# A Fourier-mixing and cosine-gated feed-forward kernel: a weight load issued once instead of twice, two last sums on GpSimd, and other queues for the last stores

## The chip, the cores and the metric

The kernel runs on one core of a Trainium2 chip. The metric is the device time of one execution in microseconds (us); the median of several executions is compared. All data are float32.

The core has a matrix engine (TensorE; PE in the profile, and PEld for its loads of weights), a vector engine (VectorE, DVE), an activation engine (ScalarE, ACT), GpSimd (POOL) and SyncE (SP), which here only issues transfers. Transfers (DMAs) are issued from the queues of SyncE, ScalarE and GpSimd, each of which goes through its instructions in order, waits included.

## The reference

```python
x: (8, 3008, 256); w_in: (256, 2048); w_out: (2048, 256)
X = np.fft.fft(x, axis=1)
X = np.fft.fft(X, axis=2)
x = X.real.reshape(24064, 256)
h = x @ w_in
g = h * np.cos(h)
out = g @ w_out
```

## The kernel before

Each of the 8 batches goes through two parts. The **transform** computes the Fourier transform over the sequence (3008 = 47 x 64) in two matrix stages. The first stage (`first_half`, eight chunks of columns) leaves its result in tiles `zs`, which `store_z` writes to a scratch array `zd` in memory; `load_z` brings it back in another order as `z`, and `second_half` multiplies that by a table `BJ` (matmuls into `pb`, line 528). The transform over the feature axis is not done on the tokens: it is folded into the weights. `fold_weights` multiplies the input weights by cosine and sine tables (matmuls into `pw`, line 597), `keep_fold` copies the result into `WC` and `WS`, and `turn_row` turns one row of it into a column by four matmuls of one column each (`pt`, line 629). The weights `w_in` are folded in four quarters of 512 columns, each once for cosine and once for sine.

The **feed-forward** part goes in steps of 256 tokens by 256 hidden columns: six token groups for each batch, eight steps in each. A step has matmuls with the folded weights (`mm1`, line 712, two halves `e`), rounding and a sine on ScalarE with VectorE around them for `h * cos(h)`, and matmuls with the output weights (`mm2`, line 803) that add up over the eight steps of a group. The steps are laid out by hand as a pipeline (`LAG` = 3): in turn `t` of the main loop one step starts, and the three before it are further along. Symmetry halves the work: a token and its mirror image are computed together, and the output weights are first combined into sums and differences (`w2_sums`). So `mm2` leaves seven partial results in the accumulators, and sums of them give the results of the tokens and of their mirrors. For all groups but the last these sums run on GpSimd (`combine_m`, by `add`, line 855) in later turns; a 32x32 block transpose on VectorE and `store_out` (line 910) write them out, first half `sg` = 0, then `sg` = 1.

The order of the work is the order of the calls; each engine's queue is in program order. The stretches around the change:

- **Head.** SyncE issues, in this order: the tables and the first quarter of `w_in`, the input of batch 0, part of `BJ`, then `load_w(1)`, `load_w2(0, 2)`, and `load_w(2)` twice (lines 273 to 277; the transfer is line 226, into the tile `wr`). Behind these in the same queue follow the stores of the first stage for chunks 4 to 7 (`store_z`, line 505; chunks 0 to 3 are on GpSimd's queue, and one store on ScalarE's), `load_z(0, 0)` (line 514), the rest of the output weights, the last quarter of `w_in`, the second set of stores and its load, and the rest of the tables. TensorE's order is: the eight chunks of the first stage, the folds of quarter 1 (sine, cosine), `turn_row(1)`, the sine fold of quarter 2, `second_half(0, 0)`; then the first feed-forward step (`seed_first`, line 698, matmuls with a single row; `mm1`; `spread_norm`, line 556, also a single row), in between the cosine fold of quarter 2. From the second token group on, a row of each group's transform goes to memory (`nd`, line 548) and comes back spread over all partitions (`nb`, line 549); ScalarE's `seed` (line 682) starts each step from it.
- **Tail.** `combine_last` does the sums of the very last group on VectorE (lines 867 to 874). `store_last` then transposes the results on TensorE (line 884) and copies them out (887 and 888); for each half `sg` it issues four stores (line 892). Just before that, in turn `n + 1`, `store_out(..., late=True)` issues the eight stores of the second half of the group before: four from SyncE, four from GpSimd.

Of the kernel before, what the change touches and what calls it, by code (L numbers as in the profile page):

```python
# [13 lines left out]
ALU = mybir.AluOpType  # L14
# [98 lines left out]
def _cols(g):  # L113

    if g == 0:
        return [(1, 64, 0), (2, 64, 64), (3, 64, 128), (0, 33, 192)]
    return [(4 * g + q, 64, 64 * q) for q in range(4)]


def _runs(g, sg):  # L120


    runs = []
    for j, n, c in _cols(g):
        a, k = c, 0
        if sg:
            a, j = 256 - c - n, (N2 - j) % N2
            if j == 0:
                a, k, n = a + 1, 33, 31
        runs.append((a // 32, j, k, n))  # L130
    return runs
# [3 lines left out]
def kernel(  # L135
# [7 lines left out]
    nc = tc.nc  # L143
# [79 lines left out]
    def load_w(q):  # L223
        cols = slice(512 * q, 512 * q + 512)
        if q < 3:
            nc.sync.dma_start(
                out=staged[q][:, 0:1024].rearrange("p (i f) -> p i f", i=2),
                in_=moe_w_in.rearrange("(i p) f -> p i f", p=128)[:, :, cols],
            )
            return  # L230
        for i in range(2):
            nc.sync.dma_start(out=wr[q][i], in_=moe_w_in[128 * i : 128 * i + 128, cols])
# [10 lines left out]
    def load_w2(f0, f1):  # L243
        nc.sync.dma_start(
            out=w2.rearrange("p (q c) -> p q c", c=ND)[:, 2 * f0 : 2 * f1],
            in_=moe_w_out.rearrange("(q p) c -> p q c", p=128)[:, 2 * f0 : 2 * f1],
        )
# [25 lines left out]
    load_bj(0, 512)  # L273
    load_w(1)
    load_w2(0, 2)
    load_w(2)
    load_w(2)
    WC = cpool.tile([128, NDFF], FP, tag="WC", name="WC")
    WS = cpool.tile([128, NDFF], FP, tag="WS", name="WS")
# [15 lines left out]
    def psum(name, tag="fft"):  # L295
        return ppool.tile([128, 512], FP, tag=tag, bufs=bank[tag], name=name)
# [297 lines left out]
    def fold_weights(e, n, tag="M"):  # L594
        pw = psum("pw", tag)
        for i in range(2):
            nc.tensor.matmul(  # L597
                pw,
                lhsT=CS[i][:, 128 * e : 128 * e + 128],
                rhs=wr[n][i],  # L600
                start=(i == 0),
                stop=(i == 1),
            )
        return e, n, pw
# [249 lines left out]
    def add(o, a, b, less):  # L854
        return nc.gpsimd.tensor_tensor(  # L855
            out=o, in0=a, in1=b, op=ALU.subtract if less else ALU.add
        )

    def combine_last(s):
        key = (s.b, s.grp)  # L860
        M5, M3 = acc[key][2], acc[key][3]
        mv = mrs.pop(key).rearrange("p (m t) -> p m t", m=7)
        outs[key] = spool.tile([128, 7 * 256], FP, tag="cb", bufs=1, name="cb")
        cv = outs[key].rearrange("p (m t) -> p m t", m=7)
        tt, stt = nc.vector.tensor_tensor, nc.vector.scalar_tensor_tensor
        more = dict(op0=ALU.mult, op1=ALU.add)
        tt(out=cv[:, 0], in0=mv[:, 0], in1=mv[:, 1], op=ALU.add)
        stt(out=cv[:, 4], in0=M5[:, 256:512], scalar=-TWO_PI, in1=mv[:, 0], **more)
        stt(out=cv[:, 6], in0=M5[:, 0:256], scalar=TWO_PI, in1=cv[:, 4], **more)
        stt(out=cv[:, 1], in0=M3[:, 0:256], scalar=TWO_PI, in1=cv[:, 6], **more)  # L870
        store_last(s, 0)
        tt(out=cv[:, 5], in0=cv[:, 4], in1=mv[:, 3], op=ALU.add)
        tt(out=cv[:, 2], in0=cv[:, 5], in1=mv[:, 2], op=ALU.add)
        stt(out=cv[:, 3], in0=M5[:, 0:256], scalar=TWO_PI, in1=cv[:, 5], **more)
        store_last(s, 1)

    def store_last(s, sg):
        cv = outs[s.b, s.grp].rearrange("p (m t) -> p m t", m=7)
        ob = spool.tile([128, 512], FP, tag="zs", bufs=4, name="ob")
        ov = ob.rearrange("t (h c j) -> t h j c", h=2, j=2)  # L880
        pos = [psum("po", "H").rearrange("t (z j c) -> t z j c", z=2, j=2)[:, 0] for _ in "ab"]
        for j in range(2):
            for h in range(2):
                nc.tensor.transpose(
                    pos[h][:, j], cv[:, 2 * sg + j, 128 * h : 128 * h + 128], ident
                )
        nc.scalar.copy(out=ov[:, 0], in_=pos[0])
        (nc.vector.tensor_copy if sg else nc.scalar.copy)(out=ov[:, 1], in_=pos[1])
        queues = (nc.sync, nc.sync, nc.scalar if sg else nc.gpsimd, nc.sync if sg else nc.gpsimd)
        for queue, (t0, j, k, m) in zip(queues, sorted(_runs(s.grp, sg))):  # L890
            h, r0 = divmod(32 * t0, 128)
            queue.dma_start(
                out=out_r[s.b, j, k : k + m, :],
                in_=ob[r0 : r0 + m, 256 * h : 256 * h + 256],
            )

    def store_out(s, sg, late=False):
        ob = spool.tile([128, 512], FP, tag="ob", bufs=2, name="ob")
        ov = ob.rearrange("p (t c) -> p t c", c=64)
        nc.vector.transpose(  # L900
            out=ov.rearrange("p t (c j) -> p j t c", j=2),
            in_=outs[s.b, s.grp][:, 512 * sg : 512 * sg + 512],
        )
        for t0, j, k, n in _runs(s.grp, sg):
            to = out_r[s.b, j].rearrange("k (q c) -> q k c", c=64)
            for i in range(0, n, 32):
                m = min(32, n - i)
                src, dst = ov[:, t0 + i // 32], to[:, k + i : k + i + m]
                if m == 32:
                    (nc.gpsimd if late and i else nc.sync).dma_start(out=dst, in_=src)  # L910
                    continue
                for q in range(4):
                    nc.sync.dma_start(out=dst[q], in_=src[32 * q : 32 * q + m])
# [6 lines left out]
    for b in range(NB):  # L920
        for g in range(NG):
            for fp in range(8):
                s = Step()
# [59 lines left out]
    n = len(steps)  # L983
# [10 lines left out]
    late = fold_weights(0, 2)  # L994
# [37 lines left out]
    for t in range(LAG, n + LAG + 1):  # L1032
# [6 lines left out]
        if t - LAG - 1 == n - 1:  # L1039
            combine_last(steps[n - 1])  # L1040
            break
# [38 lines left out]
        if step(t - LAG - 4, True):  # L1080
            store_out(step(t - LAG - 4), 0)
        if step(t - LAG - 5, True):
            if t == n - 1:
                todo.setdefault(n + 1, []).append((store_out, step(t - LAG - 5), 1, True))
            else:
                store_out(step(t - LAG - 5), 1)
# [34 lines left out]
```

## Time and profile before

| what | value |
|---|---|
| runs (three) | 1946.1, 1946.07, 1945.48 us; median 1946.07 |
| profiled execution, device time | 1945.86 us |
| its span in the trace | 1944.1 us |
| mean granted TensorE clock | 0.996 |
| busy: PE, PEld, DVE, ACT, POOL | 99%, 87%, 92%, 79%, 22% of the span |
| DMA | 89.87 MB, mean 46 GB/s |

Times in the profile are in us from the start of the span. The device time of the profiled execution is 1.8 us more than its span. A line of a timeline reads: start, duration, engine and source line, operation, written tile and read tiles, shape, count; in brackets the engine's idle time before it and what ended that. An engine with a q (SPq) is the queue that issues a transfer, not the transfer. The chain of waits is the work that ended last, followed back from the end: each piece is what the next one waited for. A matmul of a float32 tile is executed as several instructions, so four lines "x4" may stand for two calls.

### The profile page before, as it was taken

How to read it: one execution, taken by the hardware profiler on the slowest of the kernel's cores; microseconds unless marked ns; L12 is line 12 of the kernel's file. 1: busy time of each engine (PE TensorE's matmuls, PEld its weight loads, DVE VectorE, ACT ScalarE, POOL GpSimd, SP SyncE). 2: the span in 40 equal slices, each digit the busy share in tenths (PEclk: the TensorE clock that was granted, in tenths of full speed). 3: DMA queues.
4: the chain of work that ended last, by engine and by line, in shares of the span. 5: the costliest groups of instructions: out<-in, count | busy, mean ns of one | idle time of the engine just before them, and what ended most of it. 6: DMA issues, size and time to landing. Idle time of an engine off the chain costs nothing.

```text
span 1944.1 us, 30503 instructions
## 1 busy us (share of the span) xinstructions
PE 1927.7 (99%) x9508; PEld 1692.3 (87%) x9508; DVE 1780.3 (92%) x3337; ACT 1533.4 (79%) x2888; POOL 419.1 (22%) x507
## 2 busy tenths in 40 slices
PE   8999999999999999999999999999999999999998
PEld 4888899888998889988898888988889888898887
DVE  4899999999899998999989999899999999999998
ACT  3788878888788787888878788788877888788775
POOL 3522202222022211222112221122211222111101
PEclk8999999999999999999999999999999999999999
DMA  6321130012200121011211122110231100110000
GB/s 208 100 62 40 46 89 24 22 37 75 58 22 22 46 75 48 25 26 47 82 36 27 25 56 79 29 30 20 56 85 30 26 20 24 55 28 10 12 22 23
DMA packets 157864, 89.87 MB, mean 46 GB/s; under 512 B 106751, under 2 KB 151478, under 8 KB 155234
## 3 DMA queue, kind: packets, MB, share of 16 engines
q1 hardware_dynamic: 155853, 85.89, 16.4%
q0 software_dynamic: 1728, 1.95, 0.4%
q8 instruction: 76, 1.25, 0.3%
q14 instruction: 87, 0.70, 0.1%
q10 hardware_dynamic: 120, 0.08, 0.0%
HBM read 50.59 MB, written 37.27 MB: 45 GB/s over the span
## 4 chain that ended last, share of the span: by engine, by line
PE 97%; SPq 1%; DVE 1%; DMA 1%; ACT 0%; issue 0%; POOL 0%; POOLq 0%; DVEq 0%; ACTq 0%
PE M L803 58%; PE H L712 34%; PE pb L528 2%; PE pz L420 2%; SPq L196 1%; DMA wr<-in_moe_w_in_dram 1%; PE pw L597 0%; PE pz L357 0%; PE M L420 0%; PE pz L408 0%; ACT r L743 0%; DVE S L768 0%; DVE r L747 0%; DVE r L757 0%; ACT r L753 0%
## 5 line engine op out<-in xcount | busy, mean ns | idle before, releaser
L803 PE MATMUL M<-S,VX 128*128 128x256 f32 (+1 forms) x2304 | 612.3, 375 | 0.0
L803 PEld LDWEIGHTS M<-S,VX 128*128 128x128 f32 x2304 | 437.8, 190 | 49.9
L743 ACT ACTIVATE r<-H 128x512 f32<-128x512 f32 (+1 forms) x384 | 226.2, 589 | 262.0 <-DVE h L728 260.2
L753 ACT ACTIVATE r<-r 128x1024 f32<-128x1024 f32 (+1 forms) x384 | 394.7, 1028 | 22.3 <-DVE r L747 17.1
L712 PE MATMUL H<-pq,WC 128*128 128x256 f32 (+1 forms) x1536 | 394.9, 380 | 1.0 <-ACT H L682 1.0
L712 PE MATMUL H<-pq,WS 128*128 128x256 f32 (+1 forms) x1536 | 388.9, 376 | 0.3 <-ACT ew L723 0.3
L803 PE MATMUL M<-r,w 128*128 128x256 f32 (+1 forms) x1536 | 387.8, 375 | 0.0
L682 ACT ACTIVATE H<-nb,wn 128x256 f32<-128x256 f32 (+1 forms) x766 | 362.5, 473 | 16.2 <-DVE r L757 1.3
L728 DVE TENSOR_TENSOR h<-ew,H 128x512 f32<-128x512 f32 (+1 forms) x384 | 259.1, 675 | 100.8 <-PE H L712 63.1
L712 PEld LDWEIGHTS H<-pq,WC 128*128 128x128 f32 x1536 | 284.1, 190 | 52.3 <-ACT r L743 16.7
L803 PEld LDWEIGHTS M<-r,w 128*128 128x128 f32 x1536 | 300.2, 196 | 28.3 <-issue 0.5
L712 PEld LDWEIGHTS H<-pq,WS 128*128 128x128 f32 x1536 | 291.8, 190 | 34.6 <-ACT ew L723 1.3
L747 DVE SCALAR_TENSOR_TENSOR r<-r,H 128x512 f32<-128x512 f32 (+1 forms) x384 | 258.7, 674 | 26.3 <-ACT r L743 9.7
L855 POOL TENSOR_TENSOR cb<-cb,mr 128x256 f32<-128x256 f32 (+3 forms) x188 | 158.4, 853 | 521.2 <-DVE S L778 483.0
L723 ACT ACTIVATE ew<-H 128x512 f32<-128x512 f32 (+1 forms) x384 | 225.7, 588 | 56.3 <-PE H L712 47.7
L757 DVE SCALAR_TENSOR_TENSOR r<-H,r 128x512 f32<-128x512 f32 (+1 forms) x384 | 256.2, 667 | 3.9 <-ACT r L753 3.3
L747 DVE SCALAR_TENSOR_TENSOR r<-r,h 128x512 f32<-128x512 f32 (+1 forms) x384 | 259.5, 676 | 0.0
L768 DVE TENSOR_TENSOR S<-r 128x512 f32<-128x512 f32 (+1 forms) x384 | 259.1, 675 | 0.1
L757 DVE SCALAR_TENSOR_TENSOR r<-h,r 128x512 f32<-128x512 f32 (+1 forms) x384 | 258.6, 673 | 0.0
L743 ACT ACTIVATE r<-h 128x512 f32<-128x512 f32 (+1 forms) x384 | 236.2, 615 | 0.0
L803 PE MATMUL M<-S,w 128*128 128x256 f32 (+1 forms) x768 | 226.0, 376 | 0.6 <-DVE S L778 0.6
L319 POOL TENSOR_TENSOR xs<-xp 113x512 f32<-113x512 f32 x112 | 143.0, 1277 | 386.7 <-DVE S L778 383.4
(114 smaller groups left out, 1602.9 us busy)
## 6 DMA issues: line engine op xcount, KB each, us to landing
out_dram<-ob SPq DMA_DIRECT2D x724, 32.0 KB
xp<-in_x_dram SPq DMA_DIRECT2D x250, 56.0 KB
z<-zd SPq DMA_DIRECT2D x8, 1280.0 KB
zd<-zs SPq DMA_DIRECT2D x224, 40.0 KB
nb<-nd SPq DMA_DIRECT2D x40, 128.0 KB
zd<-zs SPq DMA_DIRECT2D x224, 8.0 KB
xp<-in_x_dram SPq DMA_DIRECT2D x52, 48.0 KB
wr<-in_moe_w_in_dram SPq DMA_DIRECT2D x4, 512.0 KB
```

The source lines that it names most:

```text
L319: return nc.gpsimd.tensor_tensor(out=xs2[e][0:XL], in0=xv[:, 0], in1=xv[:, 1], op=ALU.subtract if e else ALU.add,)
L682: nc.scalar.activation(out=s.H[:, u * T : u * T + T], in_=s.nb[:, 0:T], func=AF.Copy, bias=0.25, scale=wn[:, f : f + 1],)
L712: nc.tensor.matmul(s.H[:, u * T : u * T + T], lhsT=W[:, 128 * f : 128 * f + 128], rhs=s.pq[:, e * T : e * T + T], start=False, stop=True, ...
L723: nc.scalar.mul(out=s.ew[:, 0 : 2 * s.T], in_=s.H[:, 0 : 2 * s.T], mul=2.0)
L728: return nc.vector.tensor_tensor(out=s.h[:, 0 : 2 * T].rearrange("p (u t) -> p u t", u=2)[:, :, ::-1], in0=s.ew[:, 0 : 2 * T].rearrange("p ...
L743: nc.scalar.activation(out=r, in_=h, func=AF.Copy, bias=BIG, scale=1.0)
L747: nc.vector.scalar_tensor_tensor(out=r, in0=r, scalar=-BIG, in1=h, op0=ALU.add, op1=ALU.subtract)
L753: nc.scalar.activation(out=r, in_=r, func=AF.Sin, bias=0.0, scale=SIN_SCALE)
L757: nc.vector.scalar_tensor_tensor(out=r, in0=h, scalar=-0.25, in1=r, op0=ALU.add, op1=ALU.mult)
L768: return nc.vector.tensor_tensor(out=sv[:, 0:2], in0=gv[:, 2:3].to_broadcast([128, 2, T]), in1=gv[:, 0:4:3], op=ALU.subtract,)
L803: nc.tensor.matmul(acc[key][m // 2][:, 256 * (m % 2) : 256 * (m % 2) + T], lhsT=w, rhs=a, start=first, stop=s.fp == 7, skip_group_check=True,)
L855: return nc.gpsimd.tensor_tensor(out=o, in0=a, in1=b, op=ALU.subtract if less else ALU.add)
```

## The change

Three things are changed. The third quarter of the weights (`load_w(2)`) is requested once, not twice. In `combine_last` two of the sums (`cv[:, 5]` and `cv[:, 2]`) are done by GpSimd, and stand ahead of two VectorE sums in the program. The stores at the end come from other queues: of the last four (`sg` = 1) one from SyncE, two from ScalarE and one from GpSimd, instead of three from SyncE and one from ScalarE; of the eight late stores of `store_out` two from GpSimd and six from SyncE, instead of four and four.

```diff
     load_w(1)
     load_w2(0, 2)
-    load_w(2)
     load_w(2)
@@ combine_last
         tt(out=cv[:, 0], in0=mv[:, 0], in1=mv[:, 1], op=ALU.add)
         stt(out=cv[:, 4], in0=M5[:, 256:512], scalar=-TWO_PI, in1=mv[:, 0], **more)
+        add(cv[:, 5], cv[:, 4], mv[:, 3], False)
+        add(cv[:, 2], cv[:, 5], mv[:, 2], False)
         stt(out=cv[:, 6], in0=M5[:, 0:256], scalar=TWO_PI, in1=cv[:, 4], **more)
         stt(out=cv[:, 1], in0=M3[:, 0:256], scalar=TWO_PI, in1=cv[:, 6], **more)
         store_last(s, 0)
-        tt(out=cv[:, 5], in0=cv[:, 4], in1=mv[:, 3], op=ALU.add)
-        tt(out=cv[:, 2], in0=cv[:, 5], in1=mv[:, 2], op=ALU.add)
         stt(out=cv[:, 3], in0=M5[:, 0:256], scalar=TWO_PI, in1=cv[:, 5], **more)
         store_last(s, 1)
@@ store_last
-        queues = (nc.sync, nc.sync, nc.scalar if sg else nc.gpsimd, nc.sync if sg else nc.gpsimd)
+        queues = (nc.sync, nc.scalar, nc.scalar, nc.gpsimd) if sg else (nc.sync,) * 2 + (nc.gpsimd,) * 2
@@ store_out
-        for t0, j, k, n in _runs(s.grp, sg):
+        for run, (t0, j, k, n) in enumerate(_runs(s.grp, sg)):
...
-                    (nc.gpsimd if late and i else nc.sync).dma_start(out=dst, in_=src)
+                    (nc.gpsimd if late and i and run < 2 else nc.sync).dma_start(out=dst, in_=src)
```

## The prediction

> **What bounds the kernel now.** I read the page first, then the chain of waits in order of time, SyncE's own waits, the timelines of the head and of the tail, and the granted clock in stretches. Lines of the page:
>
> ```profile
> span 1944.1 us, 30503 instructions
> PE 97%; SPq 1%; DVE 1%; DMA 1%; ACT 0%; issue 0%; POOL 0%; POOLq 0%; DVEq 0%; ACTq 0%
> ```
>
> The second line is the chain that ended last: TensorE holds 97% of it, and the change leaves its matmuls alone. So it can only act where the chain leaves TensorE, at the head (SyncE and two weight loads) and after the last matmul, and on the clock at which TensorE runs. The chain at the head (start, us, what):
>
> ```profile
> 18.20 7.79 DMA wr<-in_moe_w_in_dram
> 26.05 3.69 DMA wr<-in_moe_w_in_dram
> 29.88 3.65 PE pw L597 x4
> ...
> 34.73 1.14 PE pb L528 x8
> ...
> 36.70 1.82 PE H L698 x4
> 38.52 1.80 PE H L712 x4
> 40.31 1.04 PE pn L556 x2
> 41.36 1.80 PE H L712 x4
> 43.16 3.43 PE pw L597 x4
> ...
> 49.39 1.04 PE H L712 x4
> ```
>
> The third quarter is loaded twice in a row, and the second load starts only when the first has landed (18.20 + 7.79 = 25.99). The matmuls that fold that quarter (L597) start at 29.88, after the second landing (26.05 + 3.69 = 29.74). What SyncE waited for, and what it issued:
>
> ```profile
> SPq L226 <- DMA wr<-in_moe_w_in_dram: 7.3, 1, 7.3
> SPq L505 <- DMA wr<-in_moe_w_in_dram: 1.1, 1, 1.1
> ```
>
> ```profile
> 18.20 8.22 SPq L226 DMA_DIRECT2D wr<-in_moe_w_in_dram  x2
> 26.52 3.55 SPq L505 DMA_DIRECT2D zd<-zs  x7
> 31.75 0.35 SPq L514 DMA_DIRECT2D z<-zd  x1
> ```
>
> SyncE's queue is in order, so behind the repeated load stand seven stores of the first transform (`zd`), and behind these the load `z` that the first second-half matmuls (`pb`, L528) read. One of the stores waits 1.1 us more for a weight load. From the last store's issue (26.52 + 3.55 = 30.07) to the load of `z` are 1.68 us, from that load to `pb` 2.98 us. The profile gives "issue" as releaser of `pb`; that it is the landing of `z` is my inference, because its other operand was requested long before.
>
> **The change at the head.** Removing the repeated load takes away 7.3 us of SyncE's wait. What comes next in that queue was ready earlier:
>
> ```profile
> 24.80 0.19 ACT L479 COPY zs<-mid 64x4 f32<-64x4 f32 x1
> ```
>
> ```profile
> 27.71 1.05 PE L629 MATMUL pt<-ones,nrow 1*128 1x1 f32 x8
> 52.95 1.88 PE L597 MATMUL pw<-xs,LCS 128*128 128x512 f32 x4
> ```
>
> The last of the stores' data is ready at 24.99 (24.80 + 0.19). The last store can go at about 25.0, or at 26.0 if it still waits for the one weight load; with some 0.35 us of issue, 1.68 and 2.98 us, `pb` can read `z` between 30.0 and 31.0. The fold need no longer wait for a second landing: it follows the eight small matmuls of L629 at 27.71 + 1.05 = 28.76, and at the pace of the row at 52.95 it lasts 1.85, to 30.6. So `pb` starts between 30.6 and 31.0 instead of 34.73; I take 30.95, **3.8 us earlier**. If `z` isn't what `pb` waits for, this term shrinks towards the 29.88 - 28.76 = 1.1 us of the fold's own wait.
>
> The second term is the clock. The same four matmuls of L597 take 3.65 and 3.43 us in the chain, and 1.88 at 52.95; four of L712 take 1.80, and 1.04 at 49.39. Stretches of the grid on which the granted clock changes (us; busy of PE, PEld, DVE, ACT, POOL; then PEclk):
>
> ```profile
> 12.88:16.29 3.41, 2.40 (x16) 1.45 (x16) 3.05 (x6) 0.53 (x2) 0.00 (x0) 1.00 0.64 168
> 26.53:29.94 3.41, 2.29 (x12) 1.25 (x10) 1.82 (x5) 0.84 (x2) 0.00 (x0) 1.00 0.62 183
> 29.95:33.35 3.40, 3.40 (x4) 1.00 (x4) 0.43 (x2) 0.00 (x0) 0.00 (x0) 0.50 0.09 14
> 33.36:36.77 3.41, 1.37 (x10) 1.04 (x9) 1.04 (x3) 1.17 (x2) 0.00 (x0) 1.00 1.00 334
> 36.78:40.18 3.40, 3.40 (x8) 2.20 (x8) 1.29 (x4) 0.00 (x0) 0.00 (x0) 0.50 0.83 250
> 40.19:43.59 3.40, 3.40 (x8) 2.34 (x8) 0.72 (x2) 1.45 (x3) 0.00 (x0) 0.50 0.66 190
> 43.60:47.01 3.41, 3.41 (x6) 1.62 (x5) 1.45 (x3) 1.42 (x3) 3.06 (x10) 0.50 0.58 170
> ```
>
> The clock changes at borders 3.41 us apart, by the work of the stretch before. If the small matmuls (one column in L629, one row in L698 and L556) are not counted, the stretches that lost full clock held 1.2 us (35%, an earlier fold up to 27.71) and 1.37 us (40%); the one at 12.88 kept it with 2.40 less a few tenths of small ones (60 to 70%). At half clock 36.78 (3.40 less L698's 1.8: 50%) and 40.19 (less L556's 1.04: 70%) did not bring it back, 29.95 and 43.60 (all full) did. With the change the stretch at 26.53 holds 1.2 + 1.2 us of fold, 69%: no fall at 29.94. That at 29.95 holds 0.66 of fold and 1.13 of `pb`, 53%, between a share that fell and one that held. So the clock may fall at 33.36. At stake are the five chain pieces from 36.70 to 46.6, 1.82 + 1.80 + 1.04 + 1.80 + 3.43 = 9.89 us at half clock, about 4.95 saved at full clock. If it falls at 33.36, L698 (0.83 us after `pb`'s end, at 32.9) ends at 34.4, the two L712 and L556 at 39.0, and the fold at 41.4 or 42.5, as the clock rises at 40.18 or 43.6: against 46.59 a gain of 5.2 or 4.1. If a fall comes later it costs less, if it doesn't come the gain is 8.7. Nothing in the trace ties the borders to the kernel's start, so I take the middle of the cases with one fall: 3.8 + 2.2 = **6.0 us** (4.1 to 8.7).
>
> On the clock the Trainium skill ("TensorE: Matmul & The Clock Gate", "Why this matters for your kernels") has a rule: full clock is lost after an idle window, so gaps under about 3 us are harmless. By it the changed head, whose longest gap is under 2 us, would hold full clock and the head would give 8.7. The trace disagrees in part: the fall at 29.94 came after a gap of 1.12 us behind 1.05 us of one-column matmuls.
>
> What is late next: all other loads of this phase stand on the same queue and move up with `z`. The tightest one later that I found is the row for the second token group:
>
> ```profile
> 73.28 0.35 SPq L549 DMA_DIRECT2D nb<-nd  x1
> 76.91 0.98 ACT L682 ACTIVATE H<-nb,wn 128x256 f32<-128x256 f32 x2
> ```
>
> Only 3.6 us lie between its request and its use. If the engines gain 8.7 us and the transfers ahead of it only 3.75, it could come up to 5 us late.
>
> **The change at the tail.** Rows around the end:
>
> ```profile
> 1920.00 1.42 POOL L855 TENSOR_TENSOR cb<-cb,mr 128x256 f32<-128x256 f32 x2 [3.92 <-DVE S L778]
> 1933.62 2.31 SPq L910 DMA_DIRECT2D out_dram<-ob  x4
> 1933.89 2.78 POOL L910 DMA_DIRECT2D out_dram<-ob  x4 [12.47 <-DVE ob L900]
> 1936.07 0.42 DVE L869 SCALAR_TENSOR_TENSOR cb<-M,cb 128x256 f32<-128x256 f32 x1
> 1937.73 0.42 DVE L874 SCALAR_TENSOR_TENSOR cb<-M,cb 128x256 f32<-128x256 f32 x1
> 1937.86 3.08 SPq L892 DMA_DIRECT2D out_dram<-ob  x5
> 1938.41 1.14 POOL L892 DMA_DIRECT2D out_dram<-ob  x2 [1.73 <-ACT ob L888]
> 1938.57 0.38 ACT L887 COPY ob<-po 128x256 f32<-128x256 f32 x1 [0.45 <-PE po L884]
> ```
>
> Two sums go to GpSimd, 0.71 us each by the row at 1920.00. They can start when the sum before L869 is done (about 1936.05) and end at 1937.5, against some 1937.8 on VectorE, where L874 follows them at 1937.73. L874 now waits for GpSimd's first sum (1936.8), but stands behind L870 (to 1937.0) anyway, so it starts 0.7 earlier; behind it on VectorE is only the last copy. The second sum then decides, and the last copies (L887) come 0.3 to 0.35 earlier: at 1938.25 to 1938.6. GpSimd's two stores, queued behind the sums, need it at 1938.41, 0.9 later than it is free. GpSimd is free for the sums because it issues two of the previous half's stores instead of four (1933.89 + 1.4 = 1935.3 instead of 1936.67); with all four the sums would start 0.6 late. SyncE takes these two: six issues of 0.58 end at 1937.1, before its next at 1937.86, so they cost nothing while that 0.7 us lasts.
>
> Of the last four stores SyncE issued three and ended its five at 1940.94; the span ends 3.2 later. Now SyncE issues three in all (to 1939.7), ScalarE two (about 1938.6 to 1939.75), and GpSimd its two and one more (1938.41 + 1.14 + 0.57 = 1940.1). The last issue ends 0.8 earlier. Whether a store of GpSimd lands as soon after its issue as one of SyncE these rows don't show; I take **0.6 us**, bounds 0 and 1.0.
>
> **Sum.** The profiled execution took 1945.86 us, 0.2 under the median of the runs (1946.07), within their spread: 1945.86 - 6.0 - 0.6 = 1939.3. A difference under 0.2% (3.9 us, below 1942.2 or above 1950.0) counts as no change.
>
> **Rivals.**
> - Full clock holds: the head gives 8.7, the tail 0.6: 1936.6. For it: only one stretch is in doubt. Against: 53% lies between the falls and the stretches that held, and other positions of the grid have emptier stretches. Chance 0.23. The rule above from the Trainium skill would have it so.
> - The gain is handed back at the row of 76.91 or another load: then the gain is the transfers' 3.75 plus the tail, 1941.5. For it: 3.6 us of distance; against: ScalarE's seed there is a step ahead of its matmul. 0.10.
> - The removal doesn't do what it says: `pb` isn't released by `z`, or the stores stay late for a reason that the profile hides. Left are 1.1 and 0.6: 1944.2, no change. For it: the releaser is not named. 0.11.
> - Slower: the clock, once lost in the new order, stays at half past 47. A stretch of 3.41 at half loses 1.7; from a gain of 6.6 to a loss of 3.9 are 10.5, six stretches, up to about 67: then 1949.8 or more. Against: at half clock TensorE has no gaps, and a full stretch (43.60) brought the clock back. 0.04.
>
> **How the numbers follow.** The forecast, one fall of the clock, has 0.52, and by its head of 4.1 to 7.9 lies between 1937.4 and 1941.2. With the first two rivals and the tail's bounds the range is 1936.2 to 1942.4; outside are the last two rivals and a little below. Faster: 0.52 + 0.23 + 0.08 = 0.83; same: 0.13; slower: 0.04.
>
> **What would show it.** Right: SyncE has one wait less at L226, L505 begins before 22, `z` is requested at 27 to 28, `pb` starts near 31, and L597 behind it lasts near 1.9 or 3.4 as the clock says; the last issue ends near 1940.1 less the head's gain. Wrong: `pb` still more than 3 us behind the fold, a new TensorE gap between 60 and 80, or stores of GpSimd landing last and late.

## The result and the profile after

The changed kernel takes 1939.01 us, the median of seven runs (1937.53 to 1940.65); seven runs of the kernel before in the same session had a median of 1946.07 (1945.06 to 1946.24). The ratio is 0.9965 with a 95% interval of 0.9954 to 0.9977, so about 6.8 us or 0.35% faster. The prediction, 1939.3 us, is 0.3 us off the median. That the sum comes so close is in part luck: the head gave more than was forecast in the profiled execution (8.7 us for 6.0), and the tail took time where the prediction had put a gain. That execution took 1937.53 us, the fastest of the seven.

First two lines of the page of the changed kernel, the span and the chain by engine:

```profile
span 1935.7 us, 30503 instructions
PE 98%; DVE 1%; ACT 1%; SPq 0%; issue 0%; DMA 0%; POOL 0%; POOLq 0%; DVEq 0%; ACTq 0%
```

The DMA share and most of SyncE's have left the chain. SyncE's timeline at the head (start, duration, what was issued):

```profile
18.22 0.51 SPq L226 DMA_DIRECT2D wr<-in_moe_w_in_dram  x1
21.35 4.79 SPq L504 DMA_DIRECT2D zd<-zs  x7
27.58 0.35 SPq L513 DMA_DIRECT2D z<-zd  x1
...
63.36 0.23 SPq L547 DMA_DIRECT2D nd<-pq  x1
66.30 0.35 SPq L548 DMA_DIRECT2D nb<-nd  x1
```

One issue stands where two stood, and the 7.3 us of waiting between them are gone. The seven stores begin at 21.35 instead of 26.52, and the load of `z` goes out at 27.58 instead of 31.75, 4.17 us earlier. One of the stores still waits 1.2 us for the one load of `wr`. TensorE's timeline over the same stretch:

```profile
28.75 1.98 PE L596 MATMUL pw<-wr,LCS 128*128 128x512 f32 x4
30.57 1.05 PE L527 MATMUL pb<-BJ,z 128*128 128x128 f32 x8
32.45 1.02 PE L697 MATMUL H<-pq,nrow 1*128 1x225 f32 x4 [0.83 <-DVE pq L539]
...
35.93 1.88 PE L596 MATMUL pw<-wr,LCS 128*128 128x512 f32 x4
45.91 0.93 PE L802 MATMUL M<-r,w 128*128 128x225 f32 x4
```

The fold follows the small matmuls without a gap and lasts 1.98 instead of 3.65, `pb` stands right behind it, and the second fold lasts 1.88 (3.43 in the chain of the kernel before). The first matmul with the output weights starts at 45.91; in the kernel before it starts at 54.66. Of these 8.75 us, 4.16 were gained when `pb` starts (30.57 against 34.73), and 4.59 between `pb` and that matmul (15.34 against 19.93), where the kernel before ran 10.2 us at half clock. The granted clock of the changed kernel in stretches of the grid (busy of PE, PEld, DVE, ACT, POOL, then PEclk):

```profile
30.07:33.47 3.40, 2.57 (x15) 1.77 (x13) 2.35 (x7) 1.17 (x2) 0.00 (x0) 1.00 0.95 292
33.48:36.88 3.40, 3.34 (x13) 2.23 (x14) 1.40 (x3) 1.47 (x4) 0.00 (x0) 1.00 0.84 235
```

The stretch in doubt kept full clock here. The mean clock suggests that it didn't in every run, as 0.001 of it stands for 3.9 us at half clock (0.001 x 1936 x 2): the three runs with 0.998 or 0.999 took 1937.53, 1937.62 and 1938.8 us, the four with 0.996 or 0.997 took 1939.01 to 1940.65. Where the clock fell in those four the mean doesn't say.

At the end, from the last of TensorE's sums on:

```profile
1926.62 0.59 PE L802 MATMUL M<-S,w 128*128 128x256 f32 x2
...
1927.43 1.52 POOL L854 TENSOR_TENSOR cb<-cb,mr 128x256 f32<-128x256 f32 x2 [0.91 <-DVE cb L867]
...
1929.06 1.79 SPq L891 DMA_DIRECT2D out_dram<-ob  x3
...
1929.62 1.66 POOL L891 DMA_DIRECT2D out_dram<-ob  x3 [0.68 <-ACT ob L887]
...
1930.00 1.20 ACTq L891 DMA_DIRECT2D out_dram<-ob  x2
```

The last matmul ends at 1927.21, and from there to the end of the span are 8.5 us; in the kernel before they were 8.1 (1936.00 to 1944.08). So the tail is longer by 0.45 us, although the last issue (GpSimd's, to 1931.28) comes 4.07 us after the last matmul and not 4.94 (SyncE's, to 1940.94).

From trace to trace the sum is 4.16 + 4.59 + 0.03 in the steps between - 0.45 = 8.33 us, the difference of the spans.

### The profile page after: what moved, and what is told of

It reads as the page before. It is cut to its first block, busy times and chain, and to the rows that moved or that the text cites. A ratio compares the mean times of both kernels' runs of the same rounds, so it can differ in the third digit from the quotient of the medians.

```text
span 1935.7 us, 30503 instructions
## 1 busy us (share of the span) xinstructions
PE 1920.8 (99%) x9508; PEld 1689.4 (87%) x9508; DVE 1779.8 (92%) x3335; ACT 1533.3 (79%) x2888; POOL 419.6 (22%) x508
## 3 DMA queue, kind: packets, MB, share of 16 engines
q8 instruction: 76, 1.25, 0.3%
## 4 chain that ended last, share of the span: by engine, by line
PE 98%; DVE 1%; ACT 1%; SPq 0%; issue 0%; DMA 0%; POOL 0%; POOLq 0%; DVEq 0%; ACTq 0%
PE M L802 58%; PE H L711 34%; PE pb L527 2%; PE pz L419 2%; PE pz L472 0%; PE pw L596 0%; SPq L196 0%; PE pz L356 0%; PE M L419 0%; ACT r L742 0%; DMA xp<-in_x_dram 0%; PE pz L407 0%; DVE S L767 0%; PE pt L628 0%; DVE r L746 0%
## 5 line engine op out<-in xcount | busy, mean ns | idle before, releaser
L711 PE MATMUL H<-pq,WC 128*128 128x256 f32 (+1 forms) x1536 | 393.8, 379 | 1.3 <-ACT H L681 1.3
L711 PE MATMUL H<-pq,WS 128*128 128x256 f32 (+1 forms) x1536 | 388.0, 375 | 0.3 <-ACT ew L722 0.3
L711 PEld LDWEIGHTS H<-pq,WC 128*128 128x128 f32 x1536 | 283.2, 190 | 51.6 <-ACT r L742 16.2
L711 PEld LDWEIGHTS H<-pq,WS 128*128 128x128 f32 x1536 | 291.3, 190 | 34.4 <-ACT ew L722 1.0
```

The source lines that it names most:

```text
L711: nc.tensor.matmul(s.H[:, u * T : u * T + T], lhsT=W[:, 128 * f : 128 * f + 128], rhs=s.pq[:, e * T : e * T + T], start=False, stop=True, ...
```

## Experiments

Ratios are against the kernel before, run in the same sessions (medians 1945.5 to 1946.1), with a 95% interval. Shares of a clock stretch are worked out from the timelines.

**The head alone**, the kernel before with one line less:

```diff
     load_w(2)
-    load_w(2)
```

> The kernel before with the repeated load taken out and nothing else changed (sums and stores at the end as before). If the head carries the whole gain: last matmul 4 to 9 us earlier than before, from the last matmul to the span's end 8.1 us as before (the changed kernel has 8.5), so 1938.6 us (1937.0 to 1940.4), at most 0.5 below the changed kernel. If the tail edits carried 0.6 us of the gain, as predicted: 1939.6, slower than the changed kernel. In the trace: the L505 stores begin before 22 and pb near 31.

Measured: 1936.99 us (1936.79 to 1938.82, five runs), 0.9958 (0.9946 to 0.9971). The one line gives the whole gain, and its median lies 2.0 us under the changed kernel's, more than the 0.5 that was expected; 0.45 of that is the tail (below), the rest is not explained (the two medians come from different sessions). Its profiled execution, the longest of the five (1938.82), shows the clock falling. Its clock stretches, and TensorE in them:

```profile
31.89:35.27 3.38, 2.55 (x12) 1.63 (x10) 2.12 (x6) 0.90 (x2) 0.00 (x0) 1.00 0.76 228
35.28:38.69 3.41, 3.35 (x7) 2.18 (x7) 1.04 (x3) 1.63 (x5) 0.58 (x5) 0.50 0.78 245
```

```profile
32.84 1.02 PE L697 MATMUL H<-pq,nrow 1*128 1x225 f32 x4 [0.83 <-DVE pq L539]
33.79 1.03 PE L711 MATMUL H<-pq,WC 128*128 128x225 f32 x4
34.74 0.64 PE L555 MATMUL pn<-pq,ones 1*128 1x225 f32 x2
35.45 1.87 PE L711 MATMUL H<-pq,WS 128*128 128x225 f32 x4
37.11 2.67 PE L596 MATMUL pw<-wr,LCS 128*128 128x512 f32 x4
```

TensorE is busy for 2.55 us of the first stretch, as in the changed kernel (2.57), yet here the next stretch runs at half clock. The border lies 1.8 us later (31.89 against 30.07), the work only 0.4 (L697), and so the stretch holds two sets of matmuls with one row (L697 and most of L555, 1.4 us), and only the end of `pb` and the 1.03 us of L711 besides: 1.1 us, 34%. The changed kernel's held 1.6 us (1.55 of fold and `pb` and the start of L711), 47%.

**The tail alone**, the changed kernel with the repeated load put back:

```diff
     load_w(2)
+    load_w(2)
```

> The changed kernel with the third quarter loaded twice again, so only the tail edits against before. Prediction's step: 0.6 us faster than before, 1945.5. Rival from the changed kernel's trace (GpSimd's queue ends with a drain that lasts until 3.7 us after its last store's issue, and that issue comes 0.5 later than before): from the last matmul to the span's end 8.5 us instead of 8.1, so 0.2 to 0.7 us slower, 1946.5.

Measured: 1946.44 us (1945.14 to 1947.74, eleven runs), 1.0004 (0.9995 to 1.0013). The sums on GpSimd and the spread stores bring nothing. In its trace the tail is 8.52 us, as in the changed kernel; in the trace of the head alone it is 8.07, as in the kernel before.

**Wait or bytes.** The repeated load costs SyncE a wait, and it also moves 0.5 MB beside other loads. The changed kernel with the same bytes into a tile of its own, which nothing reads:

```diff
     load_w(2)
+    spare_w = cpool.tile([128, 1024], FP, tag="spare_w", name="spare_w")
+    nc.sync.dma_start(
+        out=spare_w.rearrange("p (i f) -> p i f", i=2),
+        in_=moe_w_in.rearrange("(i p) f -> p i f", p=128)[:, :, 1024:1536],
+    )
```

> The changed kernel plus the second load of the third quarter, but into a tile of its own that nothing reads: the 512 KB are moved again, and SyncE has no reason to wait. If SyncE's wait was the cost: the zd stores are issued from 21.4 as in the changed kernel, but their data stand behind 512 KB (about 1.5 to 3 us), so pb at 32 to 33.5 and 1940 to 1942.5 us. If the extra bytes were the cost: pb near 34.7 and 1945 to 1946.5. If neither matters for z: 1939.

and with the wait, but hardly any bytes (four columns, into the tile of the load ahead):

```diff
     load_w(2)
+    nc.sync.dma_start(out=staged[2][:, 0:4], in_=moe_w_in[0:128, 1024:1028])
```

> The changed kernel plus a second load of only four columns of the third quarter into the same place: SyncE waits for the first landing as before, but only 2 KB are moved. If SyncE's wait was the cost: the zd stores from 26.5, z requested near 30, pb near 33, 1942 to 1944.5 us; the fold of the quarter itself starts near 28.8 as in the changed kernel. If the bytes were the cost: pb near 31 and 1939.

Measured: the bytes 1941.49 us (1940.31 to 1944.86, eleven runs), 0.9982 (0.9973 to 0.999); the wait 1945.82 us (1944.6 to 1946.22, eleven runs), 1.0 (0.9991 to 1.0009). SyncE with the bytes alone, and then with the wait alone:

```profile
18.76 0.97 SPq L278 DMA_DIRECT2D spare_w<-in_moe_w_in_dram  x1
20.85 7.17 SPq L509 DMA_DIRECT2D zd<-zs  x7
29.68 0.35 SPq L518 DMA_DIRECT2D z<-zd  x1
```

```profile
18.20 0.51 SPq L226 DMA_DIRECT2D wr<-in_moe_w_in_dram  x1
26.30 0.34 SPq L277 DMA_DIRECT2D wr<-in_moe_w_in_dram  x1
26.74 2.45 SPq L505 DMA_DIRECT2D zd<-zs  x7
30.87 0.35 SPq L514 DMA_DIRECT2D z<-zd  x1
```

The bytes delay the load of `z` by 2.1 us against the changed kernel (29.68 against 27.58), the wait by 3.3. The bytes are not quite without a wait, as SyncE's waits show:

```profile
SPq L509 <- DMA spare_w<-in_moe_w_in_dram: 1.0, 1, 1.0
```

The wait alone costs about as much as the whole repeated load, more than the 1942 to 1944.5 us expected of it. By medians, with the changed tail in all four: with both 1946.44, without the bytes 0.6 less, without the wait 5.0 less, with neither 7.4 less. The two costs do not add up, and the traces show the clock behind both: the profiled executions of all three kernels took 20.89 us from `pb` to the first matmul with the output weights, at half clock, while in the runs the mean clock with the bytes alone reached 0.998 in six of eleven (1940.31 to 1941.5), and with the wait it never exceeded 0.996.

**The clock, held by extra matmuls.** Does the time behind `pb` hang on how full the stretch is? The first attempt put matmuls on an idle table `VX`, with no use for the result, around L697, in the changed kernel:

```diff
+    keep_busy(1, "M", 384)
     seed_first(s0)
+    keep_busy(1, "M", 256)
```

> The changed kernel with two dummy matmuls, one of 384 columns in TensorE's gap between pb and L697 (it waits there 0.83 us for the copies) and one of 256 columns after the single-row matmuls of L697. If what differs between executions of the changed kernel (1937.5 to 1940.7) is the clock that falls or holds: the clock holds in the trace and in every run (granted clock 0.998 or more), and the times draw together at 1937.5 to 1938.7, 0.5 us being lost to the second dummy in the chain. If the spread has another cause (the late nb row, 1.3 us of ScalarE's wait): as wide as before, and some 0.5 slower.

and in the kernel before, where the same two and four more stand around the fold of quarter 2:

```diff
+    keep_busy(1, "M", 512)
     fold(1, 2)
+    keep_busy(3, "M", 512)
...
+    keep_busy(1, "M", 384)
     seed_first(s0)
+    keep_busy(1, "M", 256)
```

> The kernel before, repeated load and all, with dummy matmuls where TensorE waits at the head: one of 512 columns before the sine fold of quarter 2, three of 512 behind it, and the two of e5_fill. pb stays at 34.7 to 35. If the clock is a cost of its own: full clock from 30 to 47, from pb to the first matmul of L803 about 16 us instead of 19.9, last matmul 3.5 to 4.5 us earlier, 1941.3 to 1942.6 us. If everything hangs on the late z: 1945.5 to 1947.

Measured: 1940.64 us (1938.53 to 1943.37, seven runs), 0.9972 (0.9961 to 0.9983), and 1943.37 us (1942.48 to 1947.32, eleven runs), 0.999 (0.9981 to 0.9999). The first is spoiled, as its timeline shows:

```profile
33.36 0.88 PE L648 MATMUL pd<-VX 128*128 128x384 f32 x2 [1.25 <-DVE VX L668]
```

The extra matmul waited 1.25 us for VectorE's write of `VX`, made a gap of its own and delayed L697, and in this trace the clock fell at 35.39. But five of the seven runs had a mean clock of 0.999 and still took 1938.53 to 1940.82, so the expectation that the times draw together when the clock holds failed. In the second kernel the extra matmuls waited for the same tile (0.68 and 1.25 us in the trace), and it gained 2.8 us all the same; its trace, one of its three longest runs (1945.97), shows the clock falling at 39.31. So both were repeated with matmuls on the part of `BJ` that `pb` reads anyway; `fill(k, n)` is k matmuls of n columns. In the changed kernel one stands between `pb` and L697:

```diff
+    fill(1, 384)
     seed_first(s0)
```

> As e5_fill, but with one dummy matmul only (384 columns, between pb and L697), and its operand is the table BJ, which lies ready, so it doesn't wait for VectorE as the dummies of e5_fill did. If the clock makes the spread of the changed kernel: a clock of 0.998 or more in nearly all runs, median 1937.5 to 1938.5, L697 no later than 1.0 us after pb's end. If one dummy is too little for the clock: as the changed kernel, 1938.5 to 1939.5 with the same spread.

and in the kernel before, with its repeated load:

```diff
+    fill(1, 512)
     fold(1, 2)
+    fill(2, 512)
...
+    fill(1, 384)
     seed_first(s0)
```

> As e6_beforefill with BJ as operand: the kernel before, repeated load and all, with dummies of 512 columns before the sine fold of quarter 2, two of 512 behind it and one of 384 between pb and L697. If the clock is a cost of its own beside the late z: pb at 34.7 to 35.2, from pb to the first matmul of L803 15.5 to 17.5 us (19.9 before), median 1941.5 to 1943. If the clock follows only from the late z: 1945 to 1946.5.

Measured: 1938.44 us (1937.34 to 1939.13, five runs), 0.9961 (0.9948 to 0.9975), for the changed kernel, within its own range, so it doesn't separate the two expectations; and 1941.03 us (1940.32 to 1942.39, eight runs), 0.9975 (0.9965 to 0.9985), for the kernel before. So four matmuls that compute nothing take 4.9 us off the kernel before (1945.91 in that session) while the repeated load stays. SyncE in that kernel, and TensorE:

```profile
31.21 0.35 SPq L514 DMA_DIRECT2D z<-zd  x1
```

```profile
34.06 1.13 PE L528 MATMUL pb<-BJ,z 128*128 128x128 f32 x8 [0.97 <-DMA z<-zd]
35.03 0.81 PE L660 MATMUL pd<-BJ 128*128 128x384 f32 x2
...
39.51 1.88 PE L597 MATMUL pw<-wr,LCS 128*128 128x512 f32 x4
```

The second fold runs at full clock (1.88 against 3.43), and from `pb` to the first matmul with the output weights it takes 15.42 us, as the changed kernel does (15.34). `pb` comes 0.67 us earlier than in the kernel before (34.06, where 34.7 to 35.2 was expected); the stretch behind it is 4.51 us shorter, and later 0.55 us are lost. Here the profile names the landing of `z` as releaser of `pb`.

**The queues at the end.** In the changed kernel GpSimd's last store is the third of three. Now it gets only one, and the rest goes elsewhere:

```diff
-        queues = (nc.sync, nc.scalar, nc.scalar, nc.gpsimd) if sg else (nc.sync,) * 2 + (nc.gpsimd,) * 2
+        queues = (nc.scalar, nc.scalar, nc.sync, nc.sync) if sg else (nc.sync, nc.sync, nc.gpsimd, nc.sync)
```

> The changed kernel with the last eight stores of store_last from other queues: first half SyncE, SyncE, GpSimd, SyncE, second half ScalarE, ScalarE, SyncE, SyncE. GpSimd's last issue then ends 3.0 us after the last matmul instead of 4.1. If GpSimd's drain, 3.7 us behind its last issue, sets the end: from the last matmul to the span's end 7.4 to 7.6 us instead of 8.53, 1 us off the time. If the last landing sets it: it lands at 6.1 to 6.4 as now, and the tail stays at 8.5 to 8.7.

Measured: 1937.33 us (1936.01 to 1938.13, five runs), 0.9955 (0.9942 to 0.9967). The tail is 7.53 us in its trace, a whole us shorter than in the changed kernel, though its stores land no earlier: the last one lands 6.37 us after the last matmul, against 6.06 in the changed kernel and 6.39 in the kernel before. Its last matmul and GpSimd's last issue, and then the line at which the queues are drained, in the kernel before, in the changed kernel and in this one (after the colon: shortest, median and longest in ns, then the first and the last start; the long drain is the first to start):

```profile
1927.43 0.59 PE L802 MATMUL M<-S,w 128*128 128x256 f32 x2
...
1930.44 0.59 POOL L891 DMA_DIRECT2D out_dram<-ob  x1 [0.68 <-ACT ob L887]
```

```profile
L1116 POOLq EVENT_SEMAPHORE  x4: 17/17/17, 1943.3 to 1944.0; - x4
L1116 POOLq DRAIN  x3: 46/102/4455, 1938.8 to 1943.8; - x3
```

```profile
L1115 POOLq EVENT_SEMAPHORE  x4: 17/17/17, 1935.0 to 1935.6; - x4
L1115 POOLq DRAIN  x3: 46/106/4462, 1930.5 to 1935.5; - x3
L1115 SPq DRAIN  x3: 7/7/7, 1933.7 to 1935.2; - x3
```

```profile
L1115 POOLq EVENT_SEMAPHORE  x4: 17/17/17, 1934.8 to 1935.4; - x4
L1115 POOLq DRAIN  x3: 46/102/4122, 1930.4 to 1935.3; - x3
L1115 SPq DRAIN  x3: 7/7/7, 1934.7 to 1935.0; - x3
```

GpSimd's last issue ends at 1939.55, 1931.28 and 1931.03 in the three. Its long drain ends at 1943.3 (1938.8 + 4.46), 1935.0 and 1934.5, that is 3.75, 3.7 and 3.5 us later. GpSimd's first event behind the drain comes at 1943.3, 1935.0 and 1934.8, and the span ends 0.7 us behind that.

In the first two the event follows the drain at once, and SyncE's queue had been drained long before (at 1942.8 and 1933.7): there GpSimd's last issue sets the end, not the last landing. In this kernel the event comes 0.3 us after GpSimd's drain has ended, right behind the drain of SyncE's queue (1934.7), which comes 0.3 us behind the last landing (1934.39). So here GpSimd is no longer the last, and by the trace the last landing sets the end. The first kernel under "the parts together" bears this out: GpSimd's last issue ends 3.0 us after the last matmul as here, the last landing comes at 6.10 us instead of 6.37, and the tail is 0.25 us shorter (7.28).

**The late row.** In the changed kernel ScalarE waits for the row of the second token group, as the prediction's second rival had it. The waiting line of the changed kernel:

```profile
69.58 0.99 ACT L681 ACTIVATE H<-nb,wn 128x256 f32<-128x256 f32 x2 [1.33 <-DMA nb<-nd]
```

The row's way out (`nd`) takes 2.94 us until the load can be requested (63.36 to 66.30), against 1.15 before. It goes out 13.7 us after the last part of `BJ` was requested (49.62), where the kernel before had 22.5 us between the two; that the table loads hold it up is inferred from that. They are requested later here:

```diff
-    load_bj(1024, NJ * 128)
-    load_v()
...
-        5: ((second_half, 0, 1),),
+        5: ((second_half, 0, 1), (load_v,), (load_bj, 1024, NJ * 128)),
```

> The changed kernel with the rest of the table BJ and the table V requested only behind the second group's row (after second_half of group 1 instead of before the first step), so that this row doesn't stand behind their data. If the late row (requested 2.9 us after its store in the changed kernel, 1.2 before; ScalarE waits 1.3 us for it) costs time: 1.1 to 1.3 us between store and request, no wait of ScalarE for nb, and 0.4 to 1.0 us faster than the changed kernel: 1938.3. If TensorE has the spare time for it: 1939.0, as the changed kernel.

Measured: 1939.05 us (1937.2 to 1940.86, five runs), 0.9967 (0.9954 to 0.9979). In this trace the wait is gone, and the row takes 1.1 us. That the edit did it is not shown: with the tables requested where they were, the row takes 1.17 us in the trace of the head alone and 1.09 in that of the first kernel below. Over all traces with the tables in their place it takes 2.9 to 3.9 us in the four in which it goes out 13 to 14 us after the request of `BJ`, and 1.1 to 1.2 where that distance is 17 us or more. Over the same count of matmuls with the output weights, from the first on, the trace takes 168.36 us where the changed kernel's takes 168.83, 0.47 less, but the median doesn't show it: the spread of the runs is larger. This trace also has the plainest clock stretch of all:

```profile
32.76:36.16 3.40, 3.04 (x13) 2.12 (x14) 2.05 (x6) 0.64 (x2) 0.00 (x0) 1.00 0.84 250
36.17:39.58 3.41, 3.41 (x7) 1.78 (x6) 1.78 (x3) 1.81 (x4) 1.71 (x7) 0.50 0.70 209
```

TensorE was busy for 3.04 of 3.40 us, with 0.36 us of gaps in all and none over 0.83 us between `pb` and L697, and the clock fell. Of the 3.04, matmuls with one row (L697, L555) are 1.5; full ones are 45%.

**The parts together**: the changed kernel with the one extra matmul, and with GpSimd's single store (`sg` = 1 on ScalarE, ScalarE, SyncE, ScalarE); then also with the later table loads and one extra matmul ahead of the first chunk:

> The changed kernel with the dummy of e8_fill2 and the queues of e7_queues, where the last store of the second half goes to ScalarE instead of SyncE. By the drain of GpSimd's queue the tail is 7.2 to 7.5 us instead of 8.5; with the clock held 1936.2 (1935.5 to 1937.2). If the dummy doesn't help: 1937 to 1938, as e7_queues.

> e10_best with the same two tables requested later, and one more dummy matmul (512 columns, on the table of the first load) in TensorE's gap before the first chunk, near 13. If the row and the fall of the clock near 14 still cost something in e10_best: 1935.5 to 1936.2, granted clock 0.998 or more in all runs. If not: 1936.4, as e10_best.

Measured: 1936.4 us (1936.07 to 1938.22, five runs), 0.9953 (0.994 to 0.9965), and 1936.19 us (1935.78 to 1938.25, five runs), 0.9955 (0.9942 to 0.9969). Their tails are 7.28 and 7.29 us. Both beat the kernel before by over 9 us and have medians 2.6 and 2.8 us under the changed kernel's; from each other, from the head alone and from the kernel with the other queues they cannot be told apart.

## Why the prediction was right, and where it was not

- **SyncE's wait and `pb`: right.** Forecast 3.8 us, `pb` at 30.95, `z` requested at 27 to 28; measured 4.16, 30.57 and 27.58. The inference that `z` releases `pb` rested on no row that names it; the trace with extra matmuls does, and in the others `pb` follows the request of `z` by 2.7 to 3.0 us (3.7 in the one with later tables). In the changed kernel both sides come together: `pb` starts as the fold ends, 2.99 us after the request of `z`, and the chain of waits goes from the fold over the copies on ScalarE and VectorE to L697.
- **The clock: the mechanism right, the size spread over runs.** The 53% expected of the doubtful stretch came out as 47%, since `pb` starts while the fold's last matmul still ends, and adds only 0.89 us to it and not 1.13. That stretch held, and the gain behind `pb` was 4.59 us, near the 4.95 at stake. This execution is the rival "full clock holds"; the trace of the head alone, with one fall (17.01 us from `pb` to the first matmul with the output weights, so 2.9 gained), is the forecast, and so, by the mean clock, are the slower runs. That the median over both lies at the forecast's value is luck.
- The rule of the Trainium skill ("TensorE: Matmul & The Clock Gate", "Why this matters for your kernels"), that idle gaps under about 3 us leave the clock alone, does not hold here: with the later table loads the clock fell after a stretch with 0.36 us of gaps. What the traces show is a share of full matmuls (of more than one row and one column) in the stretch: it fell at 45% and less (45 with the later tables, 34 with the head alone, 38 to 39 before the change) and held at 47% and more (47 in the changed kernel, 48 with the other queues, 49 with one extra matmul). All 14 traces agree up to 64 us if matmuls with one row or one column are left out: the stretches that lost full clock hold at most 46%, six of them ending between 13.5 and 14.9, and those that kept it 47% or more.
- **The tail: wrong.** The failed step is "I take **0.6 us**, bounds 0 and 1.0". The working before it held roughly: GpSimd's two sums took 1.52 us (1.42 forecast), and the last issue ends 0.87 earlier (0.8). But the term took the last issue, of whichever queue, as what sets the end. In the kernels before and after it is GpSimd's, 3.7 us of drain behind it, and that one moved from 3.55 to 4.07 us after the last matmul: the third store in its queue. Measured: 0.45 us lost in the trace, outside the bounds; by the tail alone between 1 us gained and 2.5 lost. The bound "0" left out a loss without a reason for it.
- **Given back later: seen, but small.** The row came 1.33 us late for ScalarE, and the trace shows at most 0.5 us of it on TensorE, as the prediction's "a step ahead of its matmul" had it.
- **"Doesn't do what it says" and slower: not seen.** Every trace came back to full clock by 49 at the latest.

Open are the exact share at which the clock falls (46% and 47% lie close, and the ends of matmuls are modelled), whether the late row costs anything in the median, on what the length of GpSimd's drain depends (3.5 to 3.75 us), and what else spreads the runs: the kernel before with four extra matmuls took 1940.32 to 1942.39 us, all with a mean clock of 0.998 or 0.999. Part of that may be the late row: from the first matmul with the output weights to the last, the traces differ by 1.1 us (1880.83 to 1881.96).

## What to carry over

A load that is issued again into the same tile costs the queue the landing of the first, and with it everything issued behind; look in such a queue for the transfer that the critical engine needs next. When a gap at the start of a kernel closes, ask what the clock does in the stretch behind it, and count only full matmuls; a few useless matmuls in the gap are worth trying when they wait for nothing. At the end of a kernel give GpSimd's queue its last store early: its drain can end after the last landing. Once it doesn't, look at the last landing.

## What the runs showed of the hardware

- Matmuls with one row count as next to nothing for the clock: 3.04 of 3.40 us busy, half of it with one row, and the next stretch ran at 0.50. The borders are 3.41 us apart but fall elsewhere in each execution (30.07 in the changed kernel, 31.89 and 29.35 in two others, whose work lies within 0.6 us of it), so whether the clock falls differs from run to run of one kernel.
- At half clock, stretches with 43 to 75% of full matmuls did not bring full clock back, in any trace; those with 95% and more did.
- GpSimd's drain ends 3.5 to 3.75 us after its last store was issued, in all 14 traces: 3.5 with one store of the last eight on GpSimd, 3.75 with two, 3.7 with three. The last landing lies 0.9 us ahead of that end in the kernel before, 1.7 in the changed one and 0.15 with the other queues, so it is not what the drain waits for. GpSimd's own last landing lies 1.85 to 2.1 us ahead of it; whether the drain waits for that, and then takes so long, is not shown.
- With 0.5 MB more on the way the issue of seven stores took 7.17 us instead of 4.79. In it SyncE waits for landings of loads issued earlier, for the extra one too (1.0 us).
